# Entry into the S4 loop: two Y groups turned among the sums, dK in two loads off SyncE and ScalarE, chunk 2's Y tables in period 1

## Chip, cores and metric

One core of a Trainium2 chip runs the whole program in one launch. The metric is the device time in microseconds. TensorE is called PE, VectorE DVE, ScalarE ACT, GpSimd POOL and SyncE SP, as in the profile. SP, ACT and POOL issue the DMA transfers, each in its own program order.

## Reference

What is computed is the output and the gradients of a gated mix of two branches over a sequence of L = 2048 with D = 448: an S4 convolution, whose kernel K is a sum of N = 256 complex powers for each channel, and a dense layer with a squared ReLU (F = 1792).

```python
def _A_ref(u, A_re, A_im, B_re, B_im, C_re, C_im, log_dt, Dskip):
    dt = jnp.exp(log_dt)[:, None]
    logdA = dt * (A_re + 1j * A_im)
    dB = dt * (B_re + 1j * B_im)
    P = jnp.exp(logdA[:, :, None] * l[None, None, :])
    K = jnp.einsum("dn,dnl,dn->dl", Cc, P, dB).real
    # y = irfft(rfft(u) * rfft(K)), cut to L; plus u * Dskip
def _B_ref(x, w1, b1, w2, b2):
    h = jnp.einsum("bsd,df->bsf", x, w1) + b1
    r = jnp.where(h > 0, h, 0)
    return jnp.einsum("bsf,fd->bsd", r * r, w2) + b2
g = _sigmoid((x * gate_w).sum(-1, keepdims=True))
out = g * a + (1 - g) * b      # a, b: the two branches of x = A_u
# the result: out and the gradients of all inputs but B_x, from grad_out
```

## The kernel before

**Before the loop.** The sequence is transformed (fwd1, fwd2), the spectra are multiplied and turned back half way (inv1), which leaves `hd[0]` in DRAM. The last step, `sums`, is 116 small matmuls (L1036) from four loaded quarters `hss[0..3]` of `hd[0]` into six PSUM tiles; ACT copies these to SBUF (L1043), eight stores put them into `dk_d` in DRAM (L1047, L1049), and two loads bring them back as the tile `DK`, once in partitions from 0 and once from 64 (L1052, L1053). This is dK, the gradient of the convolution kernel.

**The S4 loop.** The 448 channels are 14 chunks of 32. For a chunk, DVE builds two tables of powers from a record `rec` of seeds and levels: X by `seeds_x` and `step_x` (L656, L657, L687, L688; tokens XS, X0 to X2), and Y by `seeds_y` and `build_y` (L670, L673, L679, L723; tokens YS, Y0 to Y4). ACT first spreads the record into the fields PX (L708, L711; FX0, FX1) and PY (L716, L719; FY0 to FY2). There are two X and two Y tables, used by even and odd chunks, and one PX and one PY. With both tables PE makes K for the chunk (`kgen`, L752, KM; copied out by ACT at L759, KO). For the gradients, Y is needed turned (YT): by PE transposes and ACT copies for chunk 0 (`turn_y`, L788, L789), by DMA transposes on SP for the chunks after it (`load_yt`, L778). DK is scaled for the chunk by ACT and DVE (L795, L799; SA, SV). Then follow four products Z0 to Z3 with YT (L814 on PE, L816 on ACT), two turns T0 and T1 of X (L772 on PE), two double passes P0 and P1 on DVE (L826, L827), and two sets of sums S0 and S1 on PE (L843). Z and T share one PSUM tile, psF.

**Periods.** The string PERIOD is the order written by hand: in period c the tables of chunk c are built while the gradients of chunk c - 1 run. A D in it advances the dense branch, which is cut into 127 steps: per block of 512 positions, seven first-layer steps (six and two matmuls, L904 and L907; two relus on ACT, L911; a square on DVE, L914, two steps later; a store from POOL, L912), then eight half projections (L882, L886); then 28 second-layer steps in the same way. Each period but the first has the same share of the steps.

**Entry.** The tables of chunks 0 and 1 are built ahead of the loop. Program order on each engine is the order of emission. In the part before, it is: tables of chunk 0, all fields and tables of chunk 1, then the sums with their copies and stores, the loads of DK, the four turns of chunk 0's Y, the scaling of DK, K of chunk 0, and the loop. Period 1 has eight dense steps between its Z, T, P and S, and the load of `w2n` (L1147) from POOL for the first projection. PE takes nothing out of order, so a matmul that waits holds all behind it; the same holds for ACT's copies and the DMAs that ACT issues.

Of the kernel before, what the change touches and what calls it, by code (L numbers as in the profile page):

```python
# [12 lines left out]
ACT = mybir.ActivationFunctionType  # L13
ALU = mybir.AluOpType
# [314 lines left out]
def kernel(ctx, tc, A_u, A_A_re, A_A_im, A_B_re, A_B_im, A_C_re, A_C_im, A_log_dt, A_Dskip,  # L329
# [302 lines left out]
    DK = KW[:, NA * D:].rearrange("p (a d) -> p a d", d=D)  # L632
    for h in range(2):
        G_.memset(KW[64 * h + 32:64 * h + 64, NA * D:].bitcast(fp32), 0.0)
    RB = K.t("R32", [P, 16384])
# [215 lines left out]
    w1w = KW[:, 0:7168].rearrange("p (a f) -> p a f", a=DT)  # L851
# [13 lines left out]
    lates = []  # L865

# [28 lines left out]
    def first_layer():  # L895

        rx = [SB[:, 8192:9216], SB[:, 9216:10240], hv[:, 7168:8192], st4]
        for lb in range(4):
            for jp in range(HP):
                pss = [bank(), bank()]  # L900
                for k in range(2):
                    j = 2 * jp + k
                    for dt in range(DT - 1):
                        T_.matmul(pss[k][:], lhsT=w1w[:, dt, j * P:j * P + P], rhs=UT[:, dt, 512 * lb:512 * lb + 512], start=(dt == 0), stop=False, skip_group_check=True)  # L904
                for k in range(2):
                    j, h = 2 * jp + k, slice(64 * k, 64 * k + 64)
                    T_.matmul(pss[k][:], lhsT=w1w[h, 3, j * P:j * P + P], rhs=UT[h, 3, 512 * lb:512 * lb + 512], start=False, stop=True,  # L907
                              tile_position=(64 * k, 0), skip_group_check=True)
                r = rx[(HP * lb + jp) % 4]
                for k in range(2):  # L910
                    S.activation(r[:, 512 * k:512 * k + 512], pss[k][:], ACT.Relu, bias=b1_f[:, 2 * jp + k:2 * jp + k + 1])  # L911
                G_.dma_start(pair_rows(rT_d, jp, lb), r.rearrange("p (k l) -> p k l", k=2))  # L912
                def sq(jp=jp, r=r):
                    V.tensor_tensor(out=hblk[:, 2 * jp:2 * jp + 2].rearrange("p k l -> p (k l)"), in0=r, in1=r, op=ALU.mult)  # L914
                later(sq)
                yield
# [79 lines left out]
    for q in range(4):  # L996
        K.load_hs(hd[0], q, hss[q])
    kps = [None]
# [8 lines left out]

    seeds_x(0)
# [5 lines left out]
    load_rec(1)  # L1014
    tables(0)
    fields_x(0)
    fields_x(1)
    tables_y(0)
    nc.sync.dma_start(w1w[:, 0:3], bass.AP(tensor=B_w1.tensor, offset=B_w1.offset, ap=[[F, P], [P * F, 3], [1, F]]))
    for h in range(2):  # L1020
        nc.sync.dma_start(w1w[64 * h:64 * h + 64, 3], bass.AP(tensor=B_w1.tensor, offset=B_w1.offset + 384 * F, ap=[[F, 64], [1, F]]))
    seeds_x(1)
    seeds_y(1)
    tables(1)
    for i in range(3):
        fields_y(i)
    tables_y(1)
# [7 lines left out]
    for k, (x8, g, e, gr) in enumerate(ekeys):  # L1035
        T_.matmul(tiles[e][32 * gr:32 * gr + 32, 0:D], lhsT=ct["Ew"][:, 32 * k:32 * k + 32], rhs=hss[x8 // 2][:, g, x8 % 2, :], start=(k == first[e, gr]), stop=(k == last[e, gr]),  # L1036
                  tile_position=(0, 32 * gr), skip_group_check=True)
    stA, stB = (K.t("st", [P, 4, D], bufs=2) for i in range(2))
    for e in range(6):
# [4 lines left out]
        for l in range(2 if e < 2 else 1):  # L1044
            q = G_ if (e + l) % 2 == 0 else nc.scalar
# [4 lines left out]
    for cpy in range(2):  # L1050
        qe = nc.scalar if cpy else G_
        qe.dma_start(DK[64 * cpy:64 * cpy + 40], bass.AP(tensor=dk_d, offset=0, ap=[[16 * D, 40], [D, 16], [1, D]]))  # L1052
        qe.dma_start(DK[64 * cpy + 40:64 * cpy + 41, 0], bass.AP(tensor=dk_d, offset=640 * D, ap=[[D, 1], [1, D]]))  # L1053

# [4 lines left out]
    G_.memset(zrow, 0.0)  # L1059
    nc.scalar.dma_start(bass.AP(tensor=k_d, offset=16 * 48 * D, ap=[[D, 48], [1, D]]), zrow)  # L1060
# [9 lines left out]
    rr = [hv[:, 7168:8192], st4] + [w2v[:, 1024 * i:1024 * i + 1024] for i in range(6)]  # L1070

    xst = [0]

    def spare():

        xst[0] += 1
        return K.ps("SX"[xst[0] % 2], [P, 8, P], bf16)

    YTs[0] = [turn_y(0, g, spare, False) for g in range(NG)]
    load_rec(2)  # L1080
    scale_a(0)
    scale_v(0)
    kps[0] = kgen(0)
    k_out(0, kps[0])
    PERIOD = """XS X0 YS D Z0 Y0 X1 D X2 Z1 D Y1 T0 SA D P0 LR Y2 D Z2 D Y3 Z3 FX0 Y4 FX1 D S0 FY0 T1 D FY1 FY2 KM P1 SV D D KO S1""".split()
    nd = PERIOD.count("D")

    def token(o, c):
# [8 lines left out]
        elif o == "KO":  # L1097
            if new:
                k_out(c, kps[0])
                if c < NCH - 1:  # L1100
                    YTs[c] = [load_yt(c, g) for g in range(NG)]
                release()
# [9 lines left out]
        elif o[0:2] in ("SA", "SV"):  # L1112
            if new:
                (scale_a if o == "SA" else scale_v)(c)
        elif o[0] == "X":
# [21 lines left out]
    first_steps = 8  # L1137
    Gts = []
    BUILT = ("XS", "YS", "LR", "SA", "SV", "X0", "X1", "X2", "Y0", "Y1", "Y2", "Y3", "Y4")
    for c in range(1, NCH):  # L1140
        k = 0
        for o in PERIOD:
            if o == "D":
                k += 1
                D_(first_steps * k // nd if c == 1 else first_steps + (total - first_steps) * ((c - 2) * nd + k) // (nd * (NCH - 2)))
            elif c == 1 and o == "LR":
                G_.dma_start(w2n, bass.AP(tensor=B_w2.tensor, offset=B_w2.offset, ap=[[D, P], [P * D, FT], [1, D]]))  # L1147
            elif c == 1 and o == "SV":
                token("SA", c)
                token("SV", c)  # L1150
            elif c > 1 or o not in BUILT:
                token(o, c)
# [486 lines left out]
```

## Time and profile before

| | us |
|---|---|
| median of 3 runs | 815.4 (815.0 to 815.55) |
| the profiled execution | 817.63 |
| its span on the core | 815.8 |
| PE busy | 621.9 (76%) |
| DVE busy | 625.3 (77%) |
| ACT busy | 506.0 (62%) |
| POOL busy | 163.9 (20%) |
| mean DMA rate over the span | 219 GB/s |

A row of the timeline has the start of an instruction (or a run of like ones) in us from the span's start, its length, the engine, the line of the code, the operation, and what it writes and reads; in brackets stands how long the engine sat idle before it and what ended the wait. A q behind an engine's name marks its queue, which also issues DMAs. Rows of groups have the count, the busy time and the mean length in ns. The stretch from about 180 to 231 us is the entry; the loop runs from 231 to about 570; the last 245 us are the gradients of the weights and the way back of the spectra.

### The profile page before, as it was taken

To read this page: it belongs to the slowest core of one execution; us is meant where nothing else is said; L and a number is where in the kernel's file an instruction comes from. 1 tells how busy PE (TensorE), PEld (TensorE's weight loads), DVE (VectorE), ACT (ScalarE), POOL (GpSimd) and SP (SyncE) were. 2 spreads that over 40 slices of the span, in tenths; PEclk is the share of its full clock that TensorE was granted. 3 is DMA by queue.
4 is the path that set the end of the run, shared out by engine and by line. 5 is a ranking of instruction groups with operands and counts; after the bars stand their busy time and mean duration, and the time that the engine had idled before them with its cause. 6 is when DMAs were issued, how large, how long until landed. Compare 5 with 4: busy or idle time off the path is not lost. (4 is left out here: it accounts for less than half of the span.)

```text
span 815.8 us, 16878 instructions
## 1 busy us (share of the span) xinstructions
PE 621.9 (76%) x6749; PEld 299.4 (37%) x6749; DVE 625.3 (77%) x983; ACT 506.0 (62%) x831; POOL 163.9 (20%) x264
## 2 busy tenths in 40 slices
PE   3676467653378889898978978898778788899985
PEld 1222222121234344344534443444534333444442
DVE  3795597877826999999889999998656974687353
ACT  0696567670577676677866766673675577264553
POOL 1222000042111222222321011101034311023112
PEclk9965655575689999899989999999989799799998
DMA  9978866278758577978696979996689998899972
GB/s 193 237 200 279 302 244 231 90 291 208 209 115 180 114 179 167 174 157 191 190 187 119 288 190 251 181 263 162 212 311 324 343 314 282 260 281 330 261 196 64
DMA packets 179694, 178.87 MB, mean 219 GB/s; under 512 B 116549, under 2 KB 157471, under 8 KB 179023
## 3 DMA queue, kind: packets, MB, share of 16 engines
q1 hardware_dynamic: 152632, 101.04, 50.7%
q0 software_dynamic: 17552, 56.44, 22.6%
q10 hardware_dynamic: 9430, 20.31, 7.1%
q8 instruction: 53, 0.87, 0.4%
q14 instruction: 27, 0.21, 0.1%
HBM read 83.67 MB, written 67.53 MB: 185 GB/s over the span
## 5 line engine op out<-in xcount | busy, mean ns | idle before, releaser
L816 ACT CAST P<-psF 128x1024 bf16<-128x1024 f32 x56 | 57.0, 1018 | 36.5 <-PE psF L814 35.9
L656 DVE TENSOR_TENSOR F<-X,F 128x1024 bf16<-128x1024 bf16 (+2 forms) x42 | 64.4, 1533 | 4.1 <-ACT F L711 2.4
L882 PEld LDWEIGHTS <-U 128*128 128x128 bf16 x448 | 40.0, 100 | 52.9 <-issue 15.0
L882 PE MATMUL psN<-D,U 128*128 128x448 bf16 x224 | 52.6, 372 | 6.3 <-DMA D<-in_B_w_dram 3.6
L1196 PEld LDWEIGHTS <-S 128*128 128x128 bf16 x416 | 40.2, 101 | 40.9 <-issue 13.7
L887 POOL DMA_DIRECT2D br_d<-D x32 | 17.9, 560 | 182.7 <-ACT D L886 176.2
L814 PE MATMUL psF<-R,S 41*32 41x256 bf16 x896 | 24.4, 288 | 37.0 <-DVE P L827 16.8
L1196 PE MATMUL psX<-D,S 128*128 128x449 bf16 x224 | 49.4, 365 | 1.5 <-ACT S L1202 1.5
L882 PE MATMUL psN<-S,U 128*128 128x448 bf16 x224 | 48.0, 358 | 2.5 <-DVE U L970 2.4
L826 DVE TENSOR_TENSOR M<-P,psF 128x2048 bf16<-128x2048 bf16 x28 | 34.0, 1215 | 17.1 <-PE psF L772 17.1
L1196 PE MATMUL psX<-K,S 128*128 128x448 bf16 x192 | 43.7, 374 | 1.8 <-ACT S L1199 1.8
L962 PE MATMUL psN<-S,K 128*128 128x512 bf16 x168 | 44.4, 404 | 0.0
L1187 ACT ACTIVATE S<-psN 128x1024 bf16<-128x1024 bf16 x32 | 33.0, 1030 | 14.9 <-PE psN L1183 14.8
L904 PE MATMUL psN<-S,K 128*128 128x512 bf16 x168 | 42.2, 388 | 0.0
L967 ACT ACTIVATE U<-psN 128x512 bf16<-128x512 f32 x56 | 30.8, 605 | 15.5 <-PE psN L965 11.4
L303 PE MATMUL psN<-D,cb_MI 64*128 64x448 bf16 x96 | 31.7, 514 | 9.0 <-DVE D L288 5.7
L886 ACT CAST D<-psN 128x448 bf16<-128x448 f32 x32 | 17.0, 532 | 33.7 <-PE psN L882 33.7
L657 DVE TENSOR_TENSOR X<-F 128x512 bf16<-128x512 bf16 (+2 forms) x42 | 35.6, 849 | 1.4
L772 PE MATMUL psF<-ident,X 128*128 128x128 bf16 x448 | 33.1, 232 | 4.0 <-ACT P L816 3.9
L303 PEld LDWEIGHTS <-cb_MI 64*128 64x128 bf16 x256 | 17.0, 105 | 51.9 <-issue 46.5
L265 PEld LDWEIGHTS <-M 128*64 128x64 bf16 x192 | 13.8, 133 | 60.1 <-issue 53.6
L827 DVE TENSOR_TENSOR P<-P,psF 128x2048 bf16<-128x2048 bf16 x28 | 34.2, 1221 | 1.0
(346 smaller groups left out, 1596.6 us busy)
## 6 DMA issues: line engine op xcount, KB each, us to landing
sp<-K ACTq DMA_DIRECT2D x8, 896.0 KB
dhT_d<-U SPq DMA_DIRECT2D x28, 256.0 KB
R<-sp SPq DMA_DIRECT2D x8, 896.0 KB
S<-dhT_d POOLq DMA_DIRECT2D x14, 512.0 KB, 6.8
R<-hd SPq DMA_DIRECT2D x16, 448.0 KB
S<-rT_d POOLq DMA_DIRECT2D x12, 512.0 KB, 7.0
hd<-st SPq DMA_DIRECT2D x13, 448.0 KB
rec<-rec_d POOLq DMA_DIRECT2D x11, 448.0 KB, 4.6
```

Source lines behind the costliest of these rows:

```text
L303: nc.tensor.matmul(ps[kk2][:, 0:D], lhsT=MI[r0:r0 + 64, m, :], rhs=rh[r0:r0 + 64], start=(k_ == 0), stop=(k_ == len(terms) - 1), tile_posi ...
L656: V.tensor_tensor(out=Vt[:, 0:2 * w * n], in0=run(lo, 0, [0, 2], [NA, w], [1, n]), in1=run(PX[:, 0:1], 512 * k, [2, w], [0, n], [1, 2]), o ...
L657: V.tensor_tensor(out=run(lo, n, [NA * X2, 2], [NA, X2], [1, n]), in0=run(vb, 0, [n * X2, 2], [n, X2], [1, n]), in1=run(vb, (w + X2) * n, ...
L772: T_.transpose(ps[:, t, 128 * b:128 * b + 128], Xs[c % 2][:, o_:o_ + 128], ident[:])
L816: S.copy(zbs[c, g // 2][:, :, g % 2].rearrange("p t h k n -> p t k h n"), psz[:].rearrange("p t (k h n) -> p t k h n", k=2, h=2))
L826: V.tensor_tensor(out=pr.rearrange("p t g h k n -> p t (g h k n)"), in0=zv, in1=xv, op=ALU.mult)
L827: V.tensor_tensor(out=zv, in0=zv, in1=rev_dim(xv, 1), op=ALU.mult)
L882: T_.matmul(ps[:, 0:D], lhsT=hblk[:, j, P * tt:P * tt + P], rhs=ws[:, j, :], start=(w == 1 and j == 0), stop=(j == FT - 1))
L904: T_.matmul(pss[k][:], lhsT=w1w[:, dt, j * P:j * P + P], rhs=UT[:, dt, 512 * lb:512 * lb + 512], start=(dt == 0), stop=False, skip_group_c ...
L962: T_.matmul(pss[k][:], lhsT=w2Tw[:, jp, dt, k], rhs=dblk[:, dt], start=(dt == 0), stop=False, skip_group_check=True)
L1187: S.activation(hn(i)[:, 8 * th:8 * th + 8, :], ps[:], ACT.Square if i < FT else ACT.Copy)
L1196: T_.matmul(ps[:, 0:w], lhsT=hn(i)[:, t, :], rhs=(DB2[:, t, :] if i < FT else U[:, t, 0:w]), start=(t == 0), stop=(t == LT - 1))
```

## The change

- The loads of chunk 1's record and of w1 are emitted earlier; SP's order stays as it was there.
- The sums are taken quarter by quarter, and behind the first quarter stand the turns of groups 0 and 1 of chunk 0's Y, with their ACT copies. Groups 2 and 3 are turned after the sums.
- On ACT the fields PX of chunk 1 stay ahead of the sum copies, the fields PY go behind them. Chunk 1's Y is emitted after the sums.
- Four of the eight dk stores go from ACT to SP. The loads of DK go to SP (partitions from 0) and ACT (from 64), with 48 partitions each instead of 40 and a row; the rows that nothing fills are zeroed in DRAM by a DMA from POOL. ACT's load stands behind the copies of the turns. A store of zeros into `k_d` goes from ACT to POOL.
- K of chunk 0 comes before the scaling of DK, and four dense steps come between.
- Period 1 has an order of its own, FIRST, with ten dense steps instead of eight. From the fifth on, DVE makes the second relu half (this touches three steps; the last three are projections). The DMA transposes of chunk 1's YT stand one by one behind the products that free their places. The Y table of chunk 2 is built in period 1, so period 2 builds X alone.

```diff
+    G_.dma_start(bass.AP(tensor=dk_d, offset=640 * D, ap=[[16 * D, 8], [1, 16 * D]]), KW[32:40, NA * D:])
...
-                    S.activation(r[:, 512 * k:512 * k + 512], pss[k][:], ACT.Relu, bias=b1_f[:, 2 * jp + k:2 * jp + k + 1])
+                    if k and half_dve[0]:
+                        V.tensor_scalar(out=r[:, 512 * k:512 * k + 512], in0=pss[k][:], scalar1=b1_f[:, 2 * jp + k:2 * jp + k + 1], scalar2=0.0, op0=ALU.add, op1=ALU.max)
+                    else:
+                        S.activation(r[:, 512 * k:512 * k + 512], pss[k][:], ACT.Relu, bias=b1_f[:, 2 * jp + k:2 * jp + k + 1])
...
-    for k, (x8, g, e, gr) in enumerate(ekeys):
-        T_.matmul(tiles[e][32 * gr:32 * gr + 32, 0:D], lhsT=ct["Ew"][:, 32 * k:32 * k + 32], rhs=hss[x8 // 2][:, g, x8 % 2, :], start=(k == first[e, gr]), stop=(k == last[e, gr]),
-                  tile_position=(0, 32 * gr), skip_group_check=True)
+    for q in range(4):
+        for k, (x8, g, e, gr) in enumerate(ekeys):
+            if x8 // 2 == q:
+                T_.matmul(tiles[e][32 * gr:32 * gr + 32, 0:D], lhsT=ct["Ew"][:, 32 * k:32 * k + 32], rhs=hss[q][:, g, x8 % 2, :], start=(k == first[e, gr]), stop=(k == last[e, gr]),
+                          tile_position=(0, 32 * gr), skip_group_check=True)
+        if q == 0:
+            YTs[0] += [turn_y(0, g, spare, False) for g in range(2)]
+    rec = rec1
+    fields_x(0)
+    fields_x(1)
+    seeds_x(1)
+    seeds_y(1)
+    tables(1)
...
-            q = G_ if (e + l) % 2 == 0 else nc.scalar
+            q = G_ if (e + l) % 2 == 0 else nc.sync
...
-    for cpy in range(2):
-        qe = nc.scalar if cpy else G_
-        qe.dma_start(DK[64 * cpy:64 * cpy + 40], bass.AP(tensor=dk_d, offset=0, ap=[[16 * D, 40], [D, 16], [1, D]]))
-        qe.dma_start(DK[64 * cpy + 40:64 * cpy + 41, 0], bass.AP(tensor=dk_d, offset=640 * D, ap=[[D, 1], [1, D]]))
+    for i in range(3):
+        fields_y(i)
+    tables_y(1)
...
-    YTs[0] = [turn_y(0, g, spare, False) for g in range(NG)]
+    for g in range(2, NG):
+        YTs[0].append(turn_y(0, g, spare, False))
+    for cpy in range(2):
+        (nc.sync, nc.scalar)[cpy].dma_start(DK[64 * cpy:64 * cpy + SL], bass.AP(tensor=dk_d, offset=0, ap=[[16 * D, SL], [D, 16], [1, D]]))
     load_rec(2)
-    scale_a(0)
-    scale_v(0)
     kps[0] = kgen(0)
     k_out(0, kps[0])
+    FIRST = """D D D D SA SV Z0 L0 W2 FX0 FX1 D Z1 L1 FY0 FY1 FY2 D T0 P0 KM YS Y0 Y1 Z2 L2 D S0 Z3 L3 KO Y2 D T1 P1 D SA2 SV2 Y3 Y4 D S1""".split()
...
-    first_steps = 8
+    first_steps = FIRST.count("D")
...
-        for o in PERIOD:
+        for o in FIRST if c == 1 else PERIOD:
```

The old PERIOD, which period 1 shared with the tokens of built tables left out, is unchanged for periods 2 and later:

```python
PERIOD = """XS X0 YS D Z0 Y0 X1 D X2 Z1 D Y1 T0 SA D P0 LR Y2 D Z2 D Y3 Z3 FX0 Y4 FX1 D S0 FY0 T1 D FY1 FY2 KM P1 SV D D KO S1""".split()
```

ACT's order at the end of the entry, before the change: the last of the DK loads, the eight copies of the turned Y (into R, from psX and psS), the scaling of DK (S from K) and the copy of chunk 0's K (P from psX).

```order
L1053 DMA K_177_1325<-dk_d 1x448
L1060 DMA k_d<-P_191_1552 48x448
L789 COPY R_178_1328<-psX_1559 128x1024
L789 COPY R_178_1328<-psS_1569 128x1024
L789 COPY R_178_1328<-psX_1579 128x1024
L789 COPY R_178_1328<-psS_1589 128x1024
L789 COPY R_178_1328<-psX_1599 128x1024
L789 COPY R_178_1328<-psS_1609 128x1024
L789 COPY R_178_1328<-psX_1619 128x1024
L789 COPY R_178_1328<-psS_1629 128x1024
L795 COPY S_8_163<-K_177_1325 128x4x32 x4
L759 CAST P_191_1552<-psX_1646 128x41x8
```

And with the change, at the same place:

```order
L791 COPY R_178_1329<-psS_1626 128x1024
L1090 DMA K_177_1325<-dk_d 48x7168
L761 CAST P_195_1589<-psX_1640 128x41x8
L916 ACTIVATE S_8_163<-psN_206_1770,b_f 128x512
L916 ACTIVATE S_8_163<-psN_207_1771,b_f 128x512
L916 ACTIVATE S_8_163<-psN_208_1783,b_f 128x512
L916 ACTIVATE S_8_163<-psN_209_1784,b_f 128x512
L916 ACTIVATE U_198_1592<-psN_210_1796,b_f 128x512
L916 ACTIVATE U_198_1592<-psN_211_1797,b_f 128x512
L916 ACTIVATE st_1591<-psN_212_1810,b_f 128x512
L916 ACTIVATE st_1591<-psN_213_1811,b_f 128x512
L797 COPY S_8_163<-K_177_1325 128x4x32 x4
```

The load of DK has moved from ahead of the turns' copies to behind the last of them, and eight relus of four dense steps now stand ahead of the scaling.

DVE's order in period 1, before the change: the two passes of P1, the scaling, three dense squares (U from S, from U), then period 2 with the seeds and the first step of X and the seeds of Y.

```order
L826 TENSOR_TENSOR M_182_1340<-P_191_1552,psF_1957 128x2048
L827 TENSOR_TENSOR P_191_1552<-P_191_1552,psF_1957 128x2048
L799 TENSOR_TENSOR S_8_163<-S_8_163,vw 128x32x16
L914 TENSOR_TENSOR U_194_1557<-S_8_163 128x1024 x2
L914 TENSOR_TENSOR U_194_1557<-U_194_1557 128x1024
L687 COPY X_180_1330<-rec_1639 128x128
L688 COPY X_180_1330<-rec_1639 128x128x2
L656 TENSOR_TENSOR F_181_1339<-X_180_1330,F_181_1339 128x1024
L657 TENSOR_TENSOR X_180_1330<-F_181_1339 128x256x2
L723 COPY Y_179_1329<-rec_1639 128x2x128
```

With the change, from the two passes of P0 on:

```order
L828 TENSOR_TENSOR M_182_1341<-P_195_1589,psF_1902 128x2048
L829 TENSOR_TENSOR P_195_1589<-P_195_1589,psF_1902 128x2048
L725 COPY Y_179_1330<-rec_1638 128x2x128
L672 TENSOR_TENSOR F_181_1340<-Y_179_1330,F_181_1340 128x512
L681 TENSOR_TENSOR Y_179_1330<-F_181_1340 128x128x2
L672 TENSOR_TENSOR F_181_1340<-Y_179_1330,F_181_1340 128x1024
L681 TENSOR_TENSOR Y_179_1330<-F_181_1340 128x128x4
L914 TENSOR_SCALAR U_198_1592<-psN_224_2075,b_f 128x512
L919 TENSOR_TENSOR U_198_1592<-S_8_163 128x1024
L672 TENSOR_TENSOR F_181_1340<-Y_179_1330,F_181_1340 128x256x8 x2
L681 TENSOR_TENSOR Y_179_1330<-F_181_1340 128x128x16
```

Chunk 2's Y (tile Y from rec) has moved from behind chunk 2's X to between P0 and P1 of chunk 0, with a relu half (TENSOR_SCALAR from PSUM) among it. All lines of the code behind the change are two to sixteen higher than before.

56 lines of the change are left out of this document (29 added, 27 removed).

## The prediction

> **What bounds the kernel now.** I read the page's first line, then the busy time by stretch (columns: stretch, length, busy time with instruction count of PE, its weight loads, DVE, ACT and POOL, then granted clock, DMA share and GB/s), then the timeline of each engine over the entry.
>
> ```profile
> span 815.8 us, 16878 instructions
> 207.60:221.20 13.60, 0.95 (x16) 0.83 (x15) 12.80 (x13) 7.00 (x12) 3.66 (x7) 0.66 0.64 177
> 231.00:258.00 27.00, 21.45 (x320) 9.55 (x320) 11.56 (x16) 19.21 (x29) 6.14 (x8) 0.91 0.92 190
> 258.00:282.00 24.00, 21.58 (x320) 9.96 (x316) 23.42 (x29) 14.25 (x20) 2.84 (x6) 0.89 0.45 89
> 282.00:570.00 288.00, 249.81 (x3741) 123.13 (x3740) 273.27 (x331) 199.54 (x304) 56.71 (x91) 0.96 0.87 194
> ```
>
> From period 2 on DVE sets the pace: 23.42 of 24.0 us, then 273.27 of 288. Period 1 (231 to 258) is the exception, with DVE at 11.56 of 27, and PE worked only 0.95 us between 207.6 and 221.2. So DVE work moved from period 2 to period 1 can be worth its length, and the entry has room for dense steps. What sets the entry's end:
>
> ```profile
> 206.22 0.83 ACT L708 COPY F<-M 128x768 bf16<-128x768 bf16 x1 [21.34 <-DMA M<-rec_d]
> 209.15 1.57 ACT L719 ACTIVATE F<-M 128x768 bf16<-128x768 bf16 x2
> 210.63 0.51 ACT L1043 CAST st<-psN 128x448 bf16<-128x448 f32 x1
> 214.57 0.94 ACT L1043 CAST st<-psF 128x448 bf16<-128x448 f32 x2 [0.65 <-ACT st L1043]
> 218.27 0.53 POOL L1052 DMA_DIRECT2D K<-dk_d  x1 [2.33 <-DMA dk_d<-st]
> K<-dk_d POOLq DMA_DIRECT2D x1, 560.0 KB, 9.3
> 220.18 1.01 ACT L789 COPY R<-psX 128x1024 bf16<-128x1024 bf16 x1 [4.66 <-POOL P L1059]
> 228.03 2.44 ACT L795 COPY S<-K 128x128 bf16<-128x128 bf16 x4
> 230.99 0.41 PE L814 MATMUL psF<-R,S 41*32 41x256 bf16 x16 [2.49 <-DVE S L799]
> ```
>
> Chunk 1's record lands at 206.2. ACT makes its fields (to 210.6), copies the six sums with DMA issues between them (to 215.5), issues its dK load, then copies the eight Y turns (220.2 to 228.2). dK lands at 218.3 + 9.3 = 227.6, so two waits end together, and scaling dK (2.44 us on ACT, about 0.4 on DVE) lets Z0, the first product of chunk 0, start at 230.99.
>
> **The sums with two turned groups among them.** Rows of PE and of DVE:
>
> ```profile
> 197.91 1.22 DVE L679 TENSOR_TENSOR Y<-F 128x2048 bf16<-128x2048 bf16 x1
> 196.96 0.96 PE L1036 MATMUL psN<-D,U 128*32 128x448 bf16 x8 [2.00 <-DMA D<-hd]
> 198.80 0.61 PE L1036 MATMUL psF<-D,U 128*32 128x448 bf16 x4
> 205.11 0.55 PE L1036 MATMUL psN<-P,U 128*32 128x448 bf16 x4 [0.52 <-DMA P<-hd]
> 207.01 0.54 PE L1036 MATMUL psF<-P,U 128*32 128x448 bf16 x3
> 221.24 1.01 PE L788 MATMUL psX<-ident,Y 128*128 128x128 bf16 x8 [12.68 <-ACT R L789]
> 225.46 0.65 PE L788 MATMUL psX<-ident,Y 128*128 128x128 bf16 x8 [0.18 <-ACT R L789]
> ```
>
> Chunk 0's Y is ready at 199.13 (197.91 + 1.22), so the turns, which stand behind the first quarter of the sums, start there and hold the second quarter, ready since 196.96. Two groups need 4.2 us (221.24 to 225.46 in the old place), so PE returns at about 203.3. Between the first two of these sum rows and their ends lie 24 matmuls in 2.45 us (0.10 each), between the next two the last 42 in 2.44 (0.058, partly at a rising clock). The 96 sums behind the turns take 5.6 us at the second pace, to 208.9; at half of the first, 0.05, they take 4.8, to 208.1. Before, they ended at 207.55. I take 208.2, as most of them would come at a raised clock: 0.6 us of PE, and hardly anything for ACT, which makes the X fields until 207.9 (0.83 and twice about 0.5 from 206.2).
>
> The first row of turns takes 1.01 us for eight, the one 4.2 us later 0.65: in this trace a run of transposes alone raises the clock. [...]
>
> **The dK chain.** Sum copies now come before the Y fields and without ACT's four DMA issues: six at about 0.5 us, 208.2 to 211.1. The stores go half to SyncE, behind the rest of w1 on its queue. The old last store left at 215.5 and the load at 218.3, 2.8 later; with 2.8 here the first dK load leaves at about 214, and at 218 at worst if SyncE's queue holds the stores as long as before. The second load stands on ACT behind Y fields (3.0, to 214.1) and the copies of groups 2 and 3 (4 x 1.01, to 218.2): it leaves at about 217.3 to 218, as early as before. Each load is now 48 partitions instead of 40, 672 KB. With the old 9.3 us it lands at 227; alone on the engines, with the first largely done, in 6 to 7 us, at 224. Zeros for rows 640 up come from one more POOL DMA near 184, in a stretch where POOL waited 0.86 us before its next memset: nothing.
>
> **Four dense steps ahead of Z0.** ACT's queue now puts eight relus of the four steps before scaling dK.
>
> ```profile
> 234.09 2.31 PE L904 MATMUL psN<-S,K 128*128 128x512 bf16 x6
> 239.27 1.47 PE L904 MATMUL psN<-S,K 128*128 128x512 bf16 x6
> 239.37 1.26 ACT L911 ACTIVATE U<-psN,b_f 128x512 bf16<-128x512 f32 x2 [1.35 <-PE psN L907]
> 237.82 1.22 DVE L826 TENSOR_TENSOR M<-P,psF 128x2048 bf16<-128x2048 bf16 x1 [2.21 <-PE psF L772]
> L914 DVE TENSOR_TENSOR U<-S 128x1024 bf16<-128x1024 bf16 x4 | 2.7, 685 | 4.0 <-ACT S L911 4.0
> L219 DVE CAST S<-psN 128x448 bf16<-128x448 f32 x1 | 0.6, 625 | 0.0
> D<-in_B_w_dram POOLq DMA_DIRECT2D x1, 1568.0 KB, 13.7
> ```
>
> Chunk 0's K (1.2 us) runs at 217.3, the steps from 218.6. A step is six matmuls and two small ones, 1.8 us at the full clock, 2.7 after idleness: two at 2.5 and two at 1.8 end at 227.2. Their last relus end at 228.4, later than dK on any of the above, then 2.44 + 0.4: Z0 at 231.2 against 230.99. The bounds are 229.8 (all four steps at 1.8) and 232.3 (dK at 229, should SyncE's stores be late). **Term 1: +0.2 us**, but with four of the dense steps done.
>
> **Period 1.** Z0 to chunk 0's first pass P0 on DVE: Z0 0.45, evacuation 1.0, X fields 1.7, one relu half 0.65, Z1's evacuation 1.0, turn of X 1.1: about 6.0, P0 at 237.2 (before 237.82). From there DVE runs without a gap: two P passes 2 x 2.45, chunk 2's Y in three pieces, one relu half (bounded by the 625 ns cast of 448 below and ACT's 0.65 above: 0.7), three squares 3 x 0.65, scaling 0.4. Y's lengths are those of chunk 1:
>
> ```profile
> 206.66 0.75 DVE L723 COPY R<-M 128x256 bf16<-128x256 bf16 x1
> 215.35 0.59 DVE L670 TENSOR_TENSOR F<-R,F 128x512 bf16<-128x512 bf16 x1
> 217.57 2.36 DVE L670 TENSOR_TENSOR F<-R,F 128x2048 bf16<-128x2048 bf16 x2
> 221.23 2.50 DVE L673 TENSOR_TENSOR F<-R,F 128x1024 bf16<-128x1024 bf16 x4
> 223.76 1.23 DVE L679 TENSOR_TENSOR R<-F 128x2048 bf16<-128x2048 bf16 x1
> ```
>
> That is 0.75 + 2.2, then 3.7, then 3.8, in all 10.4. Sum from P0: 4.9 + 10.4 + 0.7 + 1.95 + 0.4 = 18.35, so chunk 2's X starts at 255.5 against 255.99. **Term 2: -0.7** beyond term 1. PE is not in the way: w2 leaves POOL right behind the fourth step's store, near 229, lands 13.7 later at 243, before the first projection wants it, where it was late before. ACT keeps its fields and relus but loses three relu halves.
>
> **Period 2.** DVE and PE as they were:
>
> ```profile
> 255.99 0.44 DVE L687 COPY X<-rec 128x128 bf16<-128x128 bf16 x1
> 266.63 1.21 DVE L826 TENSOR_TENSOR M<-P,psF 128x2048 bf16<-128x2048 bf16 x1
> 269.15 0.41 PE L814 MATMUL psF<-R,S 41*32 41x256 bf16 x16 [2.42 <-DVE P L827]
> 275.06 1.07 PE L772 MATMUL psF<-ident,X 128*128 128x128 bf16 x16
> 279.05 0.44 DVE L687 COPY X<-rec 128x128 bf16<-128x128 bf16 x1
> ```
>
> X start to P0 was 10.64 and contained Y's first piece, 2.95, now gone. **Term 3: -2.95.** P0 to the next X start was 12.4, with 7.5 of Y in it; without them PE decides: from the end of P0 two Z, two dense pieces, the S sums and the turn, 7.0 us as before (269.15 to 276.13) or 6.0 at the full clock, then P1 2.45 and scaling 0.4, with P0 itself 2.45: 11.3 to 12.3. **Term 4: -0.6**, bounds 0 and -1.1. So 7.5 us of Y leave DVE, but hardly 1 is gained: PE is late next.
>
> **The rest.** Ten dense steps lie in period 1 instead of eight, so the other twelve periods share 117 instead of 119. Two steps cost DVE about 2 x 0.69 x 7/15 = 0.6 and PE 3.6; DVE being the bound, **term 5: -0.6**.
>
> **Sum:** +0.2 - 0.7 - 2.95 - 0.6 - 0.6 = -4.65 us, from the profiled execution's 817.63 (span 815.8 plus 1.8) to 813.0. The median of the runs shown is 815.4; the same -4.65 gives 810.7. Bounds of the unknown costs (Z0 1.4 earlier or 1.1 later, term 4, term 5 from 0 to -1.5) put the forecast's own range at 808.5 to 813.4.
>
> **Rivals.** (a) *Cold sums.* If the clock does not rise in the turns, the 96 sums take 9.6 us at 0.10, to 212.9: 4.7 after my 208.2. ACT's whole queue behind them, dK's second load and the four steps shift as much, Z0 to 235.9, and all but 0.0 to 0.5 of the gain goes: 815.2. The 0.65 us row is against it; for it is that those turns ran without sums ahead. Chance 0.13. [...]
>
> (b) *A worse phase in the loop, slower.* Dense steps, loads of r and writes of dh now fall at other places of each of the eleven later periods. DVE idles 14.7 us in 288, 1.3 a period:
>
> ```profile
> 407.00:432.00 25.00, 20.39 (x301) 8.91 (x300) 21.54 (x26) 17.35 (x27) 6.48 (x9) 0.86 0.90 159
> 457.00:482.00 25.00, 20.59 (x313) 9.70 (x311) 24.62 (x33) 17.64 (x29) 1.08 (x2) 1.00 1.12 289
> ```
>
> One stretch has 3.5 us of it, another 0.4, at equal work. It decides from 4.65 / 11 = 0.42 us a period; if three periods go from the one to the other, 3 x 3.1 = 9.3 minus some that go back, say 2.5, gives +6.8 - 4.65 = +2.2: 817.6. Against it: dependencies between chunks are unchanged and the shift is only a fraction of a step. Chance 0.24.
>
> (c) *More gain.* Z0 at 229.8, PE at the full clock in period 2, and PE's 3.6 us of dense work counting where it is the bound: -1.2 - 0.7 - 2.95 - 1.1 - 2 = -8.0, 807.4. For it: PE is busy 21.58 of 24.0 in period 2. Chance 0.13. That the tables don't move is excluded by the instruction order.
>
> **Numbers.** Forecast 0.50. A change of under 0.2% (1.6 us) can't be told from none here. Faster (below 813.8): forecast 0.49, (c) 0.13, (a) 0.04, together 0.66. Within: (a) 0.06, (b) 0.03, forecast 0.01, together 0.10. Slower (above 817.0): (b) 0.21, (a) 0.03: 0.24. Range 806 to 818.
>
> **What would show it.** Right: the turns at L790 start near 199 and sums (L1044) end by 209; dK's scaling (L797) starts behind the relus, near 228.5, not behind its DMA; Z0 near 231; DVE full from 237 to 262; P0 of chunk 1 near 262.5; the X seeds of chunk 3 near 274.5, and that lead of 4 to 5 us kept to the loop's end. Wrong: sums past 211, L797 released by a DMA, w2 still awaited at the first projection, chunk 3's seeds later than 277, or a lead that shrinks period by period.

## Result, and the profile after

| | before | changed |
|---|---|---|
| median of 20 runs each, us | 815.47 | 820.25 |
| lowest and highest run, us | 807.55 to 821.66 | 811.02 to 826.23 |
| span of the profiled execution, us | 815.8 | 820.5 |

The changed kernel is slower: ratio 1.0052, 95% interval 1.0029 to 1.0075. Here and below, a ratio and its interval leave out runs that took over 1.5% longer than the fastest of the same kernel. The forecast was 810.7, and its range ended at 818.

The page's first line and the busy time by stretch, with the columns and the stretches shown of before:

```profile
span 820.5 us, 16890 instructions
207.60:221.20 13.60, 8.26 (x210) 5.72 (x203) 12.62 (x14) 10.65 (x17) 3.12 (x6) 0.87 0.82 201
231.00:258.00 27.00, 22.97 (x349) 9.89 (x334) 20.03 (x26) 16.13 (x23) 3.29 (x5) 0.84 0.78 173
258.00:282.00 24.00, 17.92 (x263) 8.28 (x260) 15.67 (x19) 13.33 (x20) 3.05 (x5) 0.86 0.66 144
282.00:570.00 288.00, 243.05 (x3532) 117.70 (x3534) 267.48 (x324) 195.80 (x298) 54.05 (x88) 0.93 0.87 185
```

PE's hole in the entry is filled (8.26 us busy instead of 0.95). DVE has 20.03 instead of 11.56 in period 1. But in period 2 DVE is busy for 15.67 of 24 us only: the room that was made was not used. From 282 to 570 DVE was 5.8 us and PE 6.8 us less busy, at a granted clock of 0.93 instead of 0.96: the loop waits more. Where the difference arises, by the start of the same instruction in the two traces (X seeds at L687 and L689; the last scaling at L799 and L801 ends the loop):

| | before | changed | difference, growing by |
|---|---|---|---|
| Z0 of chunk 0 | 230.99 | 230.72 | -0.3 |
| X seeds of chunk 2 | 255.99 | 258.06 | +2.1 (+2.3) |
| P0 of chunk 1 | 266.63 | 265.93 | -0.7 (-2.8) |
| X seeds of chunk 3 | 279.05 | 280.35 | +1.3 (+2.0) |
| X seeds of chunk 6 | 357.70 | 357.63 | -0.1 (-1.4) |
| X seeds of chunk 7 | 384.48 | 388.16 | +3.7 (+3.8) |
| X seeds of chunk 8 | 410.14 | 413.13 | +3.0 (-0.7) |
| X seeds of chunk 9 | 440.51 | 447.73 | +7.2 (+4.2) |
| last scaling | 567.75 | 576.00 | +8.3 (+1.0) |
| end of the span | 815.8 | 820.5 | +4.7 (-3.6) |

The last row is the part behind the loop, which the change does not touch. It took 241.5 to 248.2 us in the fifteen traces of this study, and before's 248.05 is near the top, so its -3.6 is a matter of the two executions. The changed kernel's second trace has the last scaling at 576.02; of the kernel before there is this one trace only, so how the 4.8 us between the medians divide rests on it.

**The entry** did what was expected. Timeline of the changed kernel, rows of PE and ACT:

```profile
200.18 1.01 PE L790 MATMUL psX<-ident,Y 128*128 128x128 bf16 x8 [4.46 <-DVE Y L681]
...
209.33 0.71 PE L1044 MATMUL psF<-P,U 128*32 128x448 bf16 x4
...
226.54 1.27 ACT L916 ACTIVATE st<-psN,b_f 128x512 bf16<-128x512 f32 x2 [0.52 <-PE psN L909]
227.79 2.41 ACT L797 COPY S<-K 128x128 bf16<-128x128 bf16 x4
230.72 0.63 PE L816 MATMUL psF<-R,S 41*32 41x256 bf16 x16 [4.27 <-DVE S L801]
231.28 2.74 PE L906 MATMUL psN<-S,K 128*128 128x512 bf16 x6
```

The turns begin at 200.2 and the sums end at 210.0. Scaling dK (227.79) follows the last relus without a gap or a wait for its DMA. The last two rows were not foreseen: PE stood idle for 4.27 us, and the six matmuls of the step behind Z0 take 2.74 us, where they took 1.72 in the kernel before and 1.47 in the four steps from 219.48 on; the granted clock was 1.00 there (219.4 to 227) and is 0.50 here (230.7 to 234.5).

**Periods 1 and 2** of the changed kernel, DVE, PE and the ACT row that matters:

```profile
238.70 1.22 DVE L828 TENSOR_TENSOR M<-P,psF 128x2048 bf16<-128x2048 bf16 x1
...
251.15 0.53 ACT L888 CAST D<-psN 128x448 bf16<-128x448 f32 x1 [5.48 <-PE psN L884]
254.05 0.42 DVE L801 TENSOR_TENSOR S<-S,vw 128x512 bf16<-128x512 bf16 x1 [1.54 <-ACT S L797]
258.06 0.47 DVE L689 COPY X<-rec 128x128 bf16<-128x128 bf16 x1
...
265.93 1.22 DVE L828 TENSOR_TENSOR M<-P,psF 128x2048 bf16<-128x2048 bf16 x1
268.45 0.63 PE L816 MATMUL psF<-R,S 41*32 41x256 bf16 x16 [6.08 <-DVE P L829]
269.01 2.80 PE L884 MATMUL psN<-D,U 128*128 128x448 bf16 x7
276.42 1.22 DVE L828 TENSOR_TENSOR M<-P,psF 128x2048 bf16<-128x2048 bf16 x1 [8.02 <-PE psF L774]
279.15 0.69 DVE L919 TENSOR_TENSOR U<-st 128x1024 bf16<-128x1024 bf16 x1
279.75 0.68 DVE L919 TENSOR_TENSOR U<-S 128x1024 bf16<-128x1024 bf16 x1
280.35 0.44 DVE L689 COPY X<-rec 128x128 bf16<-128x128 bf16 x1
```

In period 1 PE waited 2.15 us at 249.59, in the middle of a projection, for squares that stand on DVE behind the 3.6 us piece Y2 (245.31 to 248.93); its next seven matmuls took 2.31 us, and ACT's copy of the projection (251.15) and with it the scaling came late. In period 2 PE waits 6.08 us for P0, which stands on DVE behind all of chunk 2's X, and comes back slowly (seven matmuls in 2.80 us, at a granted clock of 0.53 from 268 to 274; at 254.88 seven took 1.50, at 0.97 from 253 to 257). Then DVE waits 8.02 us for PE's turn of X. The two take turns instead of working side by side.

**Period 6** loses 3.8 us, **period 8** 4.2 us. They are read with the experiments that decide them.

### The profile page after: what moved, and what is told of

Its sections match the earlier page's. It is cut to its first block, busy times and chain, and to the rows that moved or that the text cites. A ratio compares the mean times of both kernels' runs of the same rounds, so it can differ in the third digit from the quotient of the medians.

```text
span 820.5 us, 16890 instructions
## 1 busy us (share of the span) xinstructions
PE 620.7 (76%) x6749; PEld 297.9 (36%) x6749; DVE 628.3 (77%) x986; ACT 504.5 (61%) x828; POOL 162.7 (20%) x264
## 5 line engine op out<-in xcount | busy, mean ns | idle before, releaser
L884 PE MATMUL psN<-D,U 128*128 128x448 bf16 x224 | 55.2, 389 | 6.2 <-DVE U L919 6.1
L884 PE MATMUL psN<-S,U 128*128 128x448 bf16 x224 | 50.7, 371 | 5.5 <-DVE U L975 5.4
L1212 PE MATMUL psX<-D,S 128*128 128x449 bf16 x224 | 47.2, 353 | 1.5 <-ACT S L1218 1.5
L774 PE MATMUL psF<-ident,X 128*128 128x128 bf16 x448 | 31.0, 224 | 4.8 <-ACT P L818 4.8
```

Of the source, the lines that this page charges most:

```text
L774: T_.transpose(ps[:, t, 128 * b:128 * b + 128], Xs[c % 2][:, o_:o_ + 128], ident[:])
L884: T_.matmul(ps[:, 0:D], lhsT=hblk[:, j, P * tt:P * tt + P], rhs=ws[:, j, :], start=(w == 1 and j == 0), stop=(j == FT - 1))
L1212: T_.matmul(ps[:, 0:w], lhsT=hn(i)[:, t, :], rhs=(DB2[:, t, :] if i < FT else U[:, t, 0:w]), start=(t == 0), stop=(t == LT - 1))
```

## Experiments

Each kernel was compared with runs of the kernel before on the same chip; "ratio" is against those. The changed kernel stands at 1.0052.

### Eight steps or ten in period 1

The first kernel is the changed one without its last two dense steps in period 1, so that the later periods meet the dense branch in the same phase as before the change; the second is the kernel before with ten steps there.

```diff
-    FIRST = """D D D D SA SV Z0 L0 W2 FX0 FX1 D Z1 L1 FY0 FY1 FY2 D T0 P0 KM YS Y0 Y1 Z2 L2 D S0 Z3 L3 KO Y2 D T1 P1 D SA2 SV2 Y3 Y4 D S1""".split()
+    FIRST = """D D D D SA SV Z0 L0 W2 FX0 FX1 D Z1 L1 FY0 FY1 FY2 D T0 P0 KM YS Y0 Y1 Z2 L2 D S0 Z3 L3 KO Y2 D T1 P1 SA2 SV2 Y3 Y4 S1""".split()
```
```diff
-    first_steps = 8
+    first_steps = 10
```

> The change as it is, but with the last two D taken out of FIRST, so that eight dense steps lie in period 1 and every later period has the dense steps that it had before the change. Theory P (phase: the loss comes from the dense branch running one to two steps ahead of the chunks, which makes PE wait for squares that stand behind Y on DVE near 373, and for transposes of Y near 433): both waits shrink to those of the kernel before, and the last scaling of dK on DVE, at 576.0 in the change and 567.8 before, comes at 565 to 568; time 0 to 3 us under the kernel before. Theory E (entry: the new order of entry and period 1 itself, its DMAs or relu halves on DVE, costs the loop time): the last scaling stays at 573 to 577 and the time 4 to 6 us above the kernel before.

> The kernel before with ten dense steps in period 1 instead of eight, spread over it, nothing else. Theory P: the loop gets the phase of the change, a stall of about 4 us near 373 to 385 and another near 433, and the last scaling of dK comes at 573 to 577 instead of 567.8; period 1 itself gets 1 to 3 us longer. Theory E: the later loop is as before, the last scaling comes at 568 to 570, only period 1 is longer.

Measured: 816.03 us, ratio 1.0010 (0.9983 to 1.0036), and 825.52 us, ratio 1.0103 (1.0050 to 1.0156). Two dense steps moved, with no other edit, cost the kernel before 1% and give the changed one 0.4% by the ratios, though the changed kernel's two intervals (1.0029 to 1.0075 and 0.9983 to 1.0036) overlap a little. Period 6 shows the phase in every trace: from P0 to P1 pass 11.4 us in all with eight steps (before and seven others), 15.5 to 16.7 in those with ten and the same order of that period (the changed kernel twice and four others).

Much of both expectations was missed. With eight steps the last scaling came at 570.31, between the two theories' places: the lead of 4.9 us over the kernel before at chunk 9's X seeds (435.66) was lost between those of chunks 11 and 12, 35.0 us apart instead of 27.6. The trace of the kernel before with ten steps is of its fastest execution, 816.19, 9 us under its median of six, so it does not show where the 1% goes. It has a second cost of its own, a wait of 6.46 us at 252.73 for the load of w2 (3.64 in the kernel before), and the stall expected near 433 is not there: period 8 takes 27.1 us.

### P0 earlier in period 2

```diff
+    SECOND = """XS X0 D Z0 D Z1 T0 P0 X1 D X2 SA D LR D Z2 D Z3 FX0 FX1 D S0 FY0 T1 D FY1 FY2 KM P1 SV D D KO S1""".split()
-        for o in FIRST if c == 1 else PERIOD:
+        for o in FIRST if c == 1 else SECOND if c == 2 else PERIOD:
```

P0 stands behind the first piece of chunk 2's X instead of the third, with Z1 and T0 ahead of it, and the dense steps between them fall otherwise too; the second of the two kernels has eight steps in period 1 as well.

> The change with an order of its own for period 2, in which chunk 1's turn T0 and passes P0 stand ahead of X's second and third step instead of behind them. In the change DVE finished X before P0 (265.9), PE waited 6.1 us for P0 and restarted at a low clock, and DVE then waited 8.0 us for the turn. If that wait is what ate the gain of the moved Y tables, P0 comes near 261, PE's Z2 waits under 2 us, and chunk 3's X seeds start at 274 to 276 instead of 280.4. With the phase of the change the later stalls remain, so by theory P the last scaling still comes 5 us or more later than in the kernel before, less the 4 to 5 us won here: about 570 to 572. If period 2 is bound by PE anyway, the seeds stay at 279 to 281.

> Both: eight dense steps in period 1 and the early P0 in period 2. By theory P with the wait in period 2 removed: chunk 3's X seeds at 271 to 275, the last scaling at 560 to 564, time 4 to 8 us under the kernel before. If the loop is held by something that starts at fixed places (DMA), the lead shrinks and the time is within 2 us of the kernel before.

Measured: 814.46 us, ratio 0.9987 (0.9958 to 1.0016), and 810.80, ratio 0.9967 (0.9939 to 0.9994). The timeline of the first:

```profile
257.24 0.48 DVE L689 COPY X<-rec 128x128 bf16<-128x128 bf16 x1
259.45 1.22 DVE L828 TENSOR_TENSOR M<-P,psF 128x2048 bf16<-128x2048 bf16 x1
...
268.40 1.22 DVE L828 TENSOR_TENSOR M<-P,psF 128x2048 bf16<-128x2048 bf16 x1 [1.03 <-PE psF L774]
274.59 0.64 DVE L689 COPY X<-rec 128x128 bf16<-128x128 bf16 x1
```

From seeds to seeds the period takes 17.35 us (274.59 - 257.24) instead of 22.29: the waits of 6.08 and 8.02 us become none and 1.03, as PE and DVE overlap again. The room that the moved Y tables left is real, but the order of the period had to be changed to use it.

### The stores of k_d beside the DMA transposes

In period 8 of the changed kernel the last product Z3 waits for the turned Y, which SP's DMA transposes bring:

```profile
410.56 19.57 SPq L780 DMA_TRANSPOSE R<-R  x4
...
422.30 2.73 POOL L765 DMA_DIRECT2D k_d<-P  x4
...
439.11 0.63 PE L816 MATMUL psF<-R,S 41*32 41x256 bf16 x16 [6.25 <-DMA R<-R]
445.00 1.22 DVE L828 TENSOR_TENSOR M<-P,psF 128x2048 bf16<-128x2048 bf16 x1 [5.35 <-PE psF L774]
```

The k_d stores (4 x 82 KB) leave while the transposes are under way. The edit lets them leave from SP, behind the four transposes; it was put on the changed kernel, and on the version with eight steps and the early P0 (that one twice), and later on the kernel before and on the changed kernel with the early P0 alone.

```diff
-        if c in (7, NCH - 1):
+        if c == NCH - 1:
+            k_store(c)
+    def k_store(c):
             c0, n = (0, 4) if c == 7 else (4, 3)
             for g in range(NG):
-                (G_ if c == 7 else (nc.sync, nc.scalar)[g % 2]).dma_start(bass.AP(tensor=k_d, offset=112 * g + 16 * c0, ap=[[48 * D, NA], [D, NY], [1, 16 * n]]),
+                (nc.sync if c == 7 else (nc.sync, nc.scalar)[g % 2]).dma_start(bass.AP(tensor=k_d, offset=112 * g + 16 * c0, ap=[[48 * D, NA], [D, NY], [1, 16 * n]]),
...
                     YTs[c] = [load_yt(c, g) for g in range(NG)]
+                if c == 7:
+                    k_store(c)
```

> The changed kernel with one edit: the four stores of k_d for chunks 0 to 7 leave from SP behind the four DMA transposes of chunk 7, instead of from POOL (where they came at 422.3 us, beside the transposes of 410.6 to 430). Theory K (the stall before Z3 at 432.9 to 439.1, 6.25 us, and the 3.7 us before Z1 at 417.0 to 420.7 come from transposes that share the DMA engines with these stores): the two waits together fall from 9.95 to under 3 us, the X seeds at 447.7 move from 7.2 us behind the kernel before to about 2 to 4 behind, and the time from 820.25 to about 816. Rival T (the transposes are late by themselves or behind the loads of r, whatever the stores do): waits of 6 us and more stay, time 819 to 821.

> The version with eight dense steps in period 1 and P0 early in period 2 (810.8 us), with the same edit of the k_d stores. Theory K: its two waits for the turned Y (2.4 us at 407.3, 6.2 us at 415.7) shrink to under 3 together, the lead of 8.5 us over the kernel before, of which 4.2 were lost in that period, is kept, and the time is about 807. Rival T: the waits stay and the time is 810 to 812.

> The version with eight steps, P0 early and k_d on SP once more, since only six runs stood behind its 807.76. If the gains of the single edits add (eight steps about 4, P0 early 5, k_d 4 to 6 us against the changed kernel), the time is 805 to 810, 5 to 10 us under the kernel before of the same call. If the one execution before was a lucky one, 810 to 813, as the version with the stores on POOL.

> The kernel before with only the k_d stores of chunks 0 to 7 moved to SP behind the transposes of chunk 7. Its own waits for the turned Y in that period are 3.1 us (Z1 at 416.1) and none before Z3. Theory K1 (the changed kernel brought the clash about, by its ten steps, which put the stores at 422.3 instead of 412.6): the gain here is 0 to 2 us, time 813.5 to 816.5. Rival K2 (the stores cost every version the same): gain 5 to 6 us as in the changed kernel, time 809 to 811.

> The changed kernel with ten steps in period 1, P0 early in period 2 and k_d on SP: one edit (two dense steps) from the 807.8 version. If the phase costs by itself (P0 to P1 near 370 to 385 takes 15 to 16 us instead of 11.4), the time is 811 to 813. If the phase only acted through the stores of k_d, it is 807 to 809.

| with k_d on SP | median, us | ratio (95%) |
|---|---|---|
| changed kernel | 815.56 | 0.9983 (0.9958 to 1.0008) |
| eight steps, P0 early | 807.76 | 0.9890 (0.9854 to 0.9925) |
| the same again | 807.47 | 0.9914 (0.9884 to 0.9944) |
| kernel before | 811.33 | 0.9945 (0.9915 to 0.9974) |
| changed, P0 early (ten steps) | 811.49 | 0.9976 (0.9948 to 1.0004) |

The timeline of the first of them at that place:

```profile
409.47 17.07 SPq L784 DMA_TRANSPOSE R<-R  x4
...
418.98 0.41 PE L820 MATMUL psF<-R,S 41*32 41x256 bf16 x16 [3.17 <-DMA R<-R]
419.32 2.73 PE L971 MATMUL psN<-S,K 128*128 128x512 bf16 x6
...
426.59 3.62 SPq L769 DMA_DIRECT2D k_d<-P  x4
...
431.17 0.41 PE L820 MATMUL psF<-R,S 41*32 41x256 bf16 x16
```

Z3 no longer waits (431.17), and the X seeds of chunk 9 come at 440.58 instead of 447.73. The wait ahead of Z1 stays (3.17 us, 3.70 without the edit). But the kernel before gains 3.6 us by the same edit, between what its two theories said (0 to 2, and 5 to 6), and its profiled execution shows no gain in that period (X seeds of chunk 9 at 441.23): with the stores out of the way, PE there still waits 4.46 us for the turned Y at 421.20. By the ratios the edit helps three versions; for the changed kernel with P0 early, 0.9987 and 0.9976 are not told apart. Whether the stores cost the changed kernel more than the old one, and so have a part in the 4.8 us, stays open. The ten steps alone do not bring the stall about: the version with eight steps and P0 early has it too (a wait of 6.24 us at 415.70, period 8 in 34.5 us), and the kernel before with ten steps, whose stores leave at 425.52 as the transposes end, has not. Eight steps against ten with the other two edits made (rows two, three and five) are 0.6 to 0.9 points: the phase costs by itself, not only through these stores.

### The tables alone

The kernel before with its own entry, and chunk 2's Y (with its fields, and K of chunk 1 ahead) in period 1, at eight steps:

```diff
+    FIRST = """D Z0 FX0 FX1 D Z1 FY0 FY1 FY2 D T0 D P0 LR KM YS Y0 Y1 D Z2 D Z3 D S0 Y2 T1 D P1 SV Y3 Y4 D D KO S1""".split()
...
-        for o in PERIOD:
+        for o in FIRST if c == 1 else PERIOD:
...
+            elif c == 1 and o in YBUILT:
+                token(o, 2)
```

> The kernel before with its own entry and eight dense steps in period 1, and only chunk 2's Y tables (with its fields, K of chunk 1 ahead of them) moved into period 1. Theory (what the changed kernel gains comes from the moved tables and the four steps ahead of Z0 together, since with eight steps in period 1 both must fit before the X seeds): period 1 gets longer by 1 to 4 us, P0 of chunk 1 comes 0 to 2 us earlier than before's 266.6, X seeds of chunk 3 at 278 to 280, time 815 to 818. Rival (the rearranged entry is worth nothing, the tables alone carry it): P0 of chunk 1 at 263 to 264 as in the changed kernel with eight steps, X seeds of chunk 3 at 276, time 814 to 816 as there.

Measured: 817.51 us, ratio 1.0009 (0.9973 to 1.0045); P0 of chunk 1 at 267.26, X seeds of chunk 3 at 278.07. With the rearranged entry (the changed kernel with eight steps) these come at 263.67 and 275.87. Period 1 got 3.4 us longer, as the first theory had it, and P0 came 0.6 us later instead of earlier. The rival fell, by one trace of each: the entry is what makes room for the tables. A part of that is the earlier load of w2, for which PE still waits 3.33 us at 255.32 here; how much was not tried. By the medians neither of the two is told from the kernel before.

### The changed kernel once more

> The changed kernel once more, for a second trace of it. If the phase of dense steps against chunks sets the two stalls, both stand at the same instructions: P0 to P1 near 375 to 385 takes 15 to 16 us (11.4 in the kernel before), and Z3 near 435 to 439 waits 4 us or more for the turned Y. If they come by chance from the DMA traffic of one execution, at most one of them is there and the others move.

One run, 824.8 us. P0 to P1 of period 6 take 15.5 us again (369.85 to 385.36), and Z3 waits 5.39 us for the turned Y at 439.78. Both stalls belong to the order, not to the execution.

### What the phase does in period 6

Timeline of the changed kernel there, DVE and PE, and then the granted clock by stretch (the third number from the right):

```profile
369.90 1.21 DVE L828 TENSOR_TENSOR M<-P,psF 128x2048 bf16<-128x2048 bf16 x1
372.43 0.44 PE L816 MATMUL psF<-R,S 41*32 41x256 bf16 x16 [2.11 <-DVE P L829]
...
375.82 0.68 DVE L919 TENSOR_TENSOR U<-U 128x1024 bf16<-128x1024 bf16 x1
376.42 0.69 DVE L919 TENSOR_TENSOR U<-st 128x1024 bf16<-128x1024 bf16 x1
...
376.56 1.68 PE L884 MATMUL psN<-D,U 128*128 128x448 bf16 x4 [2.46 <-DVE U L919]
380.29 2.78 PE L884 MATMUL psN<-D,U 128*128 128x448 bf16 x7
384.26 1.07 PE L774 MATMUL psF<-ident,X 128*128 128x128 bf16 x16
385.43 1.22 DVE L828 TENSOR_TENSOR M<-P,psF 128x2048 bf16<-128x2048 bf16 x1 [4.66 <-PE psF L774]
```

```profile
372.00:376.50 4.50, 1.67 (x19) 0.42 (x19) 4.47 (x6) 1.01 (x1) 0.19 (x1) 0.58 0.75 236
376.50:380.00 3.50, 3.44 (x29) 1.49 (x29) 3.47 (x7) 1.18 (x2) 2.00 (x3) 0.50 0.43 138
380.00:383.00 3.00, 3.00 (x10) 1.13 (x10) 0.77 (x1) 2.74 (x5) 0.00 (x0) 0.51 0.49 119
383.00:386.00 3.00, 3.00 (x46) 2.13 (x45) 0.57 (x1) 2.19 (x2) 0.00 (x0) 1.00 1.75 207
```

With ten steps the first projection of a block falls into this period right behind its last squares. The squares stand on DVE behind a 3.6 us piece of Y, PE waits 2.46 us for them in the middle of a projection, and works at half clock until 383 (0.50 and 0.51 from 376.5 on). In this one period, Y2 moved behind the next D tests it:

```diff
+    SIXTH = """XS X0 YS D Z0 Y0 X1 D X2 Z1 D Y1 T0 SA D P0 LR D Y2 Z2 D Y3 Z3 FX0 Y4 FX1 D S0 FY0 T1 D FY1 FY2 KM P1 SV D D KO S1""".split()
...
-        for o in FIRST if c == 1 else PERIOD:
+        for o in FIRST if c == 1 else SIXTH if c == 6 else PERIOD:
```

> The changed kernel with one piece of DVE work moved in period 6 alone: the two squares that stood behind the third piece of chunk 6's Y (375.8 and 376.4 us) come ahead of it. Theory (the stall from 372 to 385 is this: the second half of the projection waits 2.46 us for the squares, PE starts the next one at a low clock, 2.78 us instead of 1.5, and the turn of X and P1 are late by it): PE waits under 0.5 us there, P0 to P1 falls from 15.5 to 11.5 to 13 us, the X seeds of chunk 7 from 388.1 to about 385, the time from 820.25 to 816 to 818. Rival (the transposes of w1 that this phase puts between the products make the period long by themselves): P0 to P1 stays over 14.5 and the time at 819 to 821.

Measured: 813.56 us, ratio 0.9981 (0.9953 to 1.0008). The timeline:

```profile
368.86 1.21 DVE L828 TENSOR_TENSOR M<-P,psF 128x2048 bf16<-128x2048 bf16 x1
371.25 0.68 DVE L919 TENSOR_TENSOR U<-U 128x1024 bf16<-128x1024 bf16 x1
371.38 0.54 PE L816 MATMUL psF<-R,S 41*32 41x256 bf16 x16 [2.40 <-DVE P L829]
...
371.86 2.80 PE L884 MATMUL psN<-D,U 128*128 128x448 bf16 x7
...
376.08 1.50 PE L884 MATMUL psN<-D,U 128*128 128x448 bf16 x7
...
379.94 1.22 DVE L828 TENSOR_TENSOR M<-P,psF 128x2048 bf16<-128x2048 bf16 x1
```

P0 to P1 is 11.08 us, better than expected; P1 comes 5.5 us earlier, 1.0 of which this execution already had at P0. PE slows behind P0 here too (2.40 us idle, then seven matmuls in 2.80 us, at a granted clock of 0.54 from 371.3 to 374.5), but the next projection runs in 1.50: what the edit removes is the second wait and the slow stretch behind it. Swapping two squares with one Y piece, in one period of thirteen, takes back the change's loss by the medians. In its trace the lead of 2.5 us over the kernel before at chunk 8's X seeds (407.64) is gone at chunk 9's (440.45), in the period of the k_d stores. The phase costs through this collision on DVE; the turns of w1 that the rival blamed are still there (eight transposes behind each half projection).

### The stores of dh from POOL

The version with eight steps, P0 early and k_d on SP, the fastest one, loses 7 us later: X seeds of chunks 11 and 12 lie 34.8 us apart in its first trace (477.62 to 512.45), 27.6 in the kernel before. In its second trace:

```profile
474.80 20.48 SPq L784 DMA_TRANSPOSE R<-Y  x4
495.37 0.53 SPq L980 DMA_DIRECT2D dhT_d<-U  x1
...
498.39 1.08 ACT L976 ACTIVATE U<-psN 128x512 bf16<-128x512 f32 x2 [5.96 <-DMA dhT_d<-U]
```

The dh stores stand on SP behind the transposes, and ACT waits for them to free its tile.

```diff
-                    behind.append(lambda: nc.sync.dma_start(pair_rows(dhT_d, jp, lb), hb))
+                    behind.append(lambda: G_.dma_start(pair_rows(dhT_d, jp, lb), hb))
```

> The version with eight steps, P0 early and k_d on SP (807.8 us), with the stores of dh leaving from POOL instead of from SP behind the four DMA transposes (there they stood from 475.0 to 495.2, and ACT waited 5.8, 1.0 and 2.4 us for them near 492 to 504). Theory: the period that took 34.8 us there (27.6 in the kernel before) falls to 26 to 28, the time to 800 to 803. Rival: the loads of r, which stay on SP behind the same transposes, hold DVE's products instead, the period stays over 32, and the time at 806 to 809.

Measured: 815.39 us, ratio 1.0019 (0.9988 to 1.0051): 8 us worse than without the edit, and both theories missed the time.

```profile
433.56 5.37 POOL L980 DMA_DIRECT2D dhT_d<-U  x7
...
441.55 0.63 PE L820 MATMUL psF<-R,S 41*32 41x256 bf16 x16 [4.16 <-DMA R<-Y]
...
541.57 0.63 PE L820 MATMUL psF<-R,S 41*32 41x256 bf16 x16 [7.82 <-DMA R<-R]
```

The period in question did fall to 27.2 us (490.23 to 517.40), but in other periods seven stores now run beside the transposes, and the products wait longer for these (two such waits above, in periods that took 31.4 and 33.6 us). That the stores delay them is read from this trace and was not tried by itself. The 7 us of the fast version are left where they are; its neighbour with k_d on POOL did not have them, as the four transposes took 13.64 us there instead of 20.48 and ACT waited 2.10 us instead of 5.96. The changed kernel with eight steps, also with k_d on POOL, has both again (20.91 us, and ACT waits 8.44), so it comes without the k_d edit too; what makes these transposes long is not settled.

## Why the prediction was wrong

- **Term 1 (Z0, +0.2):** right; Z0 came 0.3 us earlier. Sums ended at 210.0, in an execution that was 0.9 us later from 189 on (the end of chunk 0's X table), and dK was there before ACT asked. Two errors cancel in it: the four steps began at 219.48 and not 218.6, but all ran at 1.47 us for six matmuls (granted clock 1.00 from 219.4 to 227), where I had two slow steps. Rival (a) did not happen: the granted clock was 0.65 from 204.1 to 206, right behind the turns, and 1.00 from 206 to the sums' end. During the turns themselves (200 to 204.1) it stayed at 0.50, so what I read from the 0.65 us row, that a run of turns alone raises the clock, did not show there; it rose in the sums.
- **Term 2 (period 1, -0.7):** wrong, +2.3. From Z0 to P0 I took 6.0 us, and it took 7.98 (238.70 - 230.72). I filled PE's hole ahead of Z0 but left it idle for the 4.27 us of the last relus and the scaling, and Z0, Z1 and a step then ran at half clock (0.63, 0.63 and, for its six matmuls, 2.74 us; granted clock 0.50 from 230.7 to 234.5). From P0 to the X seeds I took 18.35 and it was 19.36: the scaling on ACT stands behind a projection's copy that waited 5.48 us for PE, so DVE waited 1.54. I had written "PE is not in the way" and had no term for that copy, nor for the squares behind Y2 that hold PE.
- **Term 3 (-2.95):** right; 10.64 became 7.87, so -2.8.
- **Term 4 (-0.6):** the sign was wrong, +2.0. I had seen that "PE is late next" and still priced PE's chain from P0 at 6.0 to 7.0 us, by the old trace, where PE had waited only 2.42 us ahead of it and then lost a part of its pace (seven matmuls in 2.38 us, against 1.50 at 265.23). Now it waited 6.08, ran its first products and projection at half pace (0.63, 2.80 and 0.63 us; granted clock 0.53 from 268 to 274), and the chain took 7.9 us (268.45 to 276.31). Two squares (1.2 us) ahead of the next X seeds were not in my sum at all. Moving P0 forward, which no term considered, takes 4.9 us off this period.
- **Term 5 (-0.6):** this is the step that failed most. I priced the two steps moved out of the loop by the work that they take from each period, and the loop got 6.95 us longer (8.25 at its end, less 1.3 at its start). Rival (b) named the place, dense steps that "now fall at other places of each of the eleven later periods", and its price of +6.8 for the loop, but I held it at 0.24 because "the shift is only a fraction of a step". That is wrong by the kernel's own formula for the steps: the dense branch runs two whole steps ahead in periods 2 to 5, one in periods 6 to 9, and as before from period 10 on. Even one step is enough if by it one short producer falls behind one long piece in an engine's written order, as the squares of 0.68 and 0.69 us (from 375.82) do on DVE behind 3.6 us of Y (from 372.29): 3.8 us are lost in period 6 alone, and there it is shown. The 4.2 us of period 8 are a wait for DMA transposes, which moving the k_d stores removes in the changed kernel; that this wait grew by the change is seen in two traces but not separated from what the kernel before pays there, and its cause stays open.

The errors of the terms are -0.5, +3.0, +0.2, +2.6 and +7.6 us, and -3.6 behind the loop; with the forecast sum of -4.65 they make the +4.7 of the two spans. The forecast's own range of 808.5 to 813.4 does not come out of its bounds either: added up, they give 807.9 to 813.0.

## What to carry to other kernels

When work is taken off the engine that bounds a stage, write down what stands in order ahead of the instruction that the next engine waits for, and move that instruction too; otherwise the two engines can take turns and the room is lost, as with the waits of 6.08 and 8.02 us in period 2 here. A table of an order written by hand is tuned to the phase of everything that runs through it (here two dense steps moved, with no other edit, cost the kernel before 1%), so a change in how many steps go ahead is costed by looking in each later period for a short producer that now falls behind a long piece of work. Before a wait for a DMA is blamed on its own size, look what stores were issued beside it, and try them behind it on the same queue; in period 8 of the changed kernel that removed a wait of 6.25 us.

## What the runs showed of the hardware

PE lost its clock after short idle times, but not after all of one length. In the changed kernel, after 2.11 us (372.43) and then 2.46 us (376.56), the granted clock was 0.50 to 0.58 from 372 to 383, with PE busy without a break from 376.6 on. After 3.17 us (418.98 in the changed kernel with k_d on SP) the first product still ran in 0.41 us, its full pace, but the six matmuls behind it took 2.73 us instead of 1.47, and the granted clock from 420 to 422 was 0.50. After 3.57 us in the same trace (533.60) nothing was lost: 0.41 us, then 1.47, at 1.00. After 1.83 us in the changed kernel (296.07) the first product took 0.41 us and the next seven matmuls 1.98; after 1.96 us in the kernel before (372.90) it was 0.41 and 1.50. So in these traces the first product behind a wait does not tell whether the clock is gone, and the length of the idle time alone does not settle it.

In the profiled executions of the kernel before and the changed kernel, the four DMA transposes of a period took SP 9.24 us (from 438.50, changed) to 22.11 us (from 231.57, before), from the first to the end of the last, and all that stands behind them on SP (the stores of dh, the loads of r) leaves that much later: in the second trace of the fastest version the transposes ended at 495.28, and the first dh store behind them left at 495.37.
